# Memory attention and SSM convolution on one core: two stages in a row against one interleaved program

## The chip, the cores and the metric

The kernel runs on one core of one Trainium2 chip. The metric is the device time of one execution in microseconds (us); the median of three runs stands for it. The engines are PE (TensorE, the matrix engine; PEld is its weight load), DVE (VectorE), ACT (ScalarE), POOL (GpSimd) and SP (SyncE), whose queue issues all DMAs of this kernel.

## What is computed

The reference computes two things that don't depend on each other and puts them side by side in the output (1, 2048, 1152), all in bf16.

Part A is attention with a compressive memory: x is 2048 x 576, with 32 heads of 18 channels, in 4 segments of 512 rows.

```
q, k, v = x @ wq, x @ wk, x @ wv            # per head and segment
for s in range(4):
    a_dot = softmax(q_s k_s^T * 18**-0.5 + causal mask) v_s
    a_mem = (phi(q_s) M) / (phi(q_s) z + 1e-6)   # phi(t) = t+1 if t>0 else exp(t)
    o_s   = g * a_mem + (1 - g) * a_dot          # g = sigmoid(beta) per head
    M, z  = M + phi(k_s)^T v_s, z + sum phi(k_s)
out_A = o @ wo
```

Part B is a gated long convolution over 2048 rows and 576 channels: `kv = shift_conv4(k) * v`, `y = causal_conv(kv, ssm_k) + kv * ssm_D`, `out_B = q * y`.

## The kernel before

The entry function runs `part_b` to its end and then `PartA`; each has its own pools. The order on every engine is made by the tile framework: it takes the operations in the order in which the program emits them as priority, and gives buffers from the pools as they come free.

*Part B* (L36 to L307). Tables of sines and cosines are built on DVE and ACT (L91 to L163, helper L28 to L33), seven of 128 x 17 x 128. k and v come in by transposing DMAs (L75, L76); the short convolution is 80 matmuls with diagonal weights (L182), the product with v runs on DVE (L184), and kv goes to a DRAM scratch (L187). The long convolution is a transform of length 4096 = 16 x 256 in matmuls. It runs over NG = 2 groups of GB = 288 channels, each in stages for the whole group: first transform of ssm_k (`f1`, L222, evacuated in turn by DVE L209 and ACT L207), its 17 frequency rows k1 (`f2_mm`, L233 to L240, with a row matmul L237 that adds ssm_D) into H_sb, the same for kv, where each row's product with H_sb goes into Y4 (DVE L259, L262; or ACT L265 and POOL L266), then for all 17 rows the inverse (L272 to L281) into C_sb, transposes (L293), the last small transform (L301) and the product with q (L303). PSUM: 3 tiles of 2 banks and 2 of 1.

*Part A* (L315 to L646). Weights wq and wk are loaded and padded on POOL from 18 to 32 columns a head (`pad_w`, L342 to L348), so that each head starts at a partition that is a multiple of 32. Two heads' groups of four make a pair; there are 4 segments x 4 pairs = 16 slots. `proj_qk` (L419) makes q, k and f = phi(q) of a pair: two blocks each of five matmuls for q (L428) and k (L439), the fifth with 64 rows; `proj_v` (L444) makes v, `proj_phik` (L455) projects k again with rows on partitions and makes phi(k); `mem_update` (L473) sums the memory. `scores` (L489) makes the score blocks (L497), their exp (L501, ACT) and the causal mask (L504, POOL). `av` (L537) multiplies with v (L551) and the memory (L556), evacuates (L553, L557) and normalises: eight DMAs gather the sums (cs, L564), DVE inverts (L573 to L579), eight DMAs write the inverses to DRAM (L585), four read them back broadcast (rb, L588), DVE multiplies (L591 to L594). `out_proj` (L597) multiplies with wo (L604) and stores. `slot` (L617) emits scores of pair i, projections of pair i + 2, `av` of pair i - 1, then the rest. PSUM: 2 tiles of 2 banks for scores, 4 of 1 bank for all else.

Of the kernel before, what the change touches and what calls it, by code (L numbers as in the profile page):

```python
# [13 lines left out]
I32 = dt.int32  # L14
# [21 lines left out]
def part_b(ctx, tc, B_q, B_k, B_v, B_shift_k, B_ssm_k, B_ssm_D, out, GB=288):  # L36
    nc = tc.nc
    ov = out[0].rearrange('(j p) c -> p j c', p=P)
    NG = D // GB
    consts = ctx.enter_context(tc.tile_pool(name="b_consts", bufs=1))  # L40
    ps_mm = ctx.enter_context(tc.tile_pool(name="b_ps_mm", bufs=3, space=PSUM))
    ps_sm = ctx.enter_context(tc.tile_pool(name="b_ps_sm", bufs=2, space=PSUM))

    ident = consts.tile([P, P], BF16)
    nc.gpsimd.memset(ident[:], 0.0)
    nc.gpsimd.affine_select(out=ident[:], in_=ident[:], compare_op=ALU.not_equal, fill=1.0, base=0,
                            pattern=[[-1, P]], channel_multiplier=1)
    pcol_i = consts.tile([P, 1], I32)
    nc.gpsimd.iota(pcol_i[:], pattern=[[0, 1]], base=0, channel_multiplier=1)
    pcol_f = consts.tile([P, 1], F32)  # L50
    nc.vector.tensor_copy(out=pcol_f[:], in_=pcol_i[:])
    pm16_i = consts.tile([P, 1], I32)
    nc.vector.tensor_single_scalar(out=pm16_i[:], in_=pcol_i[:], scalar=15, op=ALU.bitwise_and)
    pm16_f = consts.tile([P, 1], F32)
    nc.vector.tensor_copy(out=pm16_f[:], in_=pm16_i[:])

    ones_row = consts.tile([1, P], BF16)
    nc.vector.memset(ones_row[:], 1.0)
    d_row = consts.tile([1, D], BF16)
    nc.sync.dma_start(out=d_row[:], in_=B_ssm_D.rearrange("(o c) -> o c", o=1))  # L60

    CT0 = [0, 128, 256, 384, 448]
    kv_dram = tc.dram_tile([D, S], BF16, name="kv_scratch")
    kvctx = ExitStack()
    kvp = kvctx.enter_context(tc.tile_pool(name="b_kv", bufs=1))
    sk_bf = kvp.tile([P, 5, 4], BF16)
    for ct in range(5):
        nc.sync.dma_start(out=sk_bf[:, ct, :], in_=B_shift_k[CT0[ct]:CT0[ct] + P, :])
    kTs, vTs = [], []
    for ct in range(5):  # L70
        c0 = CT0[ct]
        kT = kvp.tile([P, KPAD + S], BF16, tag="kT%d" % ct, name="kT%d" % ct)
        vT = kvp.tile([P, S], BF16, tag="vT%d" % ct, name="vT%d" % ct)
        nc.gpsimd.memset(kT[:, 0:KPAD], 0.0)
        nc.sync.dma_start_transpose(out=kT[:, KPAD:KPAD + S], in_=B_k[0, :, c0:c0 + P])  # L75
        nc.sync.dma_start_transpose(out=vT[:, :], in_=B_v[0, :, c0:c0 + P])  # L76
        kTs.append(kT)
        vTs.append(vT)

    genctx = ExitStack()  # L80
    gen = genctx.enter_context(tc.tile_pool(name="b_gen", bufs=1))
    NK1 = 17
    CS = consts.tile([P, NK1, P], BF16)
    SN = consts.tile([P, NK1, P], BF16)
    NSN = consts.tile([P, NK1, P], BF16)
    CST = consts.tile([P, NK1, P], BF16)
    SNT = consts.tile([P, NK1, P], BF16)
    NSNT = consts.tile([P, NK1, P], BF16)
    NCST = consts.tile([P, NK1, P], BF16)
    fpat = gen.tile([P, NK1, P], I32, tag="gen_i")  # L90
    nc.gpsimd.iota(fpat[:], pattern=[[1, NK1], [32, P]], base=0, channel_multiplier=0)  # L91
    prod_f = gen.tile([P, NK1, P], F32, tag="gen_f")
    nc.vector.tensor_scalar(out=prod_f[:], in0=fpat[:], scalar1=pcol_f[:, 0:1], scalar2=None, op0=ALU.mult)
    _trig_from_idx(nc, gen, CS[:], prod_f[:], 1024, 4096, [P, NK1, P], "gen_t")
    _trig_from_idx(nc, gen, SN[:], prod_f[:], 0, 4096, [P, NK1, P], "gen_t")
    _trig_from_idx(nc, gen, NSN[:], prod_f[:], 2048, 4096, [P, NK1, P], "gen_t")
    jpat = gen.tile([P, NK1, P], I32, tag="gen_i")
    nc.gpsimd.iota(jpat[:], pattern=[[0, NK1], [1, P]], base=0, channel_multiplier=0)
    colk_i = consts.tile([P, NK1], I32)
    nc.gpsimd.iota(colk_i[:], pattern=[[1, NK1]], base=0, channel_multiplier=32)  # L100
    colk_f = consts.tile([P, NK1], F32)
    nc.vector.tensor_copy(out=colk_f[:], in_=colk_i[:])
    prodT_f = gen.tile([P, NK1, P], F32, tag="gen_f")
    for k1 in range(NK1):
        nc.vector.tensor_scalar(out=prodT_f[:, k1, :], in0=jpat[:, k1, :], scalar1=colk_f[:, k1:k1 + 1],
                                scalar2=None, op0=ALU.mult)
    _trig_from_idx(nc, gen, CST[:], prodT_f[:], 1024, 4096, [P, NK1, P], "gen_t")
    _trig_from_idx(nc, gen, SNT[:], prodT_f[:], 0, 4096, [P, NK1, P], "gen_t")
    _trig_from_idx(nc, gen, NSNT[:], prodT_f[:], 2048, 4096, [P, NK1, P], "gen_t")
    _trig_from_idx(nc, gen, NCST[:], prodT_f[:], 3072, 4096, [P, NK1, P], "gen_t")  # L110

    k1pat = gen.tile([P, 8, 32], I32, tag="w1_i")
    nc.gpsimd.iota(k1pat[:, :, 0:17], pattern=[[0, 8], [1, 17]], base=0, channel_multiplier=0)
    nc.gpsimd.iota(k1pat[:, :, 17:32], pattern=[[0, 8], [1, 15]], base=1, channel_multiplier=0)
    w1prod = gen.tile([P, 8, 32], F32, tag="w1_f")
    nc.vector.tensor_scalar(out=w1prod[:], in0=k1pat[:], scalar1=pm16_f[:, 0:1], scalar2=None, op0=ALU.mult)
    nc.vector.tensor_scalar(out=w1prod[:, :, 0:17], in0=w1prod[:, :, 0:17], scalar1=8.0, scalar2=None, op0=ALU.add)
    nc.vector.tensor_scalar(out=w1prod[:, :, 17:32], in0=w1prod[:, :, 17:32], scalar1=16.0, scalar2=None, op0=ALU.add)
    W1bd = consts.tile([P, 8, 32], BF16)
    _trig_from_idx(nc, gen, W1bd[:], w1prod[:], 0, 32, [P, 8, 32], "w1_t")  # L120
    nc.gpsimd.affine_select(out=W1bd[:], in_=W1bd[:], compare_op=ALU.is_ge, fill=0.0, base=0,
                            pattern=[[-16, 8], [0, 32]], channel_multiplier=1)
    nc.gpsimd.affine_select(out=W1bd[:], in_=W1bd[:], compare_op=ALU.is_ge, fill=0.0, base=15,
                            pattern=[[16, 8], [0, 32]], channel_multiplier=-1)

    row_i = consts.tile([P, 1], I32)
    nc.vector.tensor_single_scalar(out=row_i[:], in_=pcol_i[:], scalar=2, op=ALU.arith_shift_right)
    row_f = consts.tile([P, 1], F32)
    nc.vector.tensor_copy(out=row_f[:], in_=row_i[:])
    jj_i = consts.tile([P, 1], I32)  # L130
    nc.vector.tensor_single_scalar(out=jj_i[:], in_=pcol_i[:], scalar=3, op=ALU.bitwise_and)
    jj_f = consts.tile([P, 1], F32)
    nc.vector.tensor_copy(out=jj_f[:], in_=jj_i[:])
    rm16_i = consts.tile([P, 1], I32)
    nc.vector.tensor_single_scalar(out=rm16_i[:], in_=row_i[:], scalar=15, op=ALU.bitwise_and)
    rm16_f = consts.tile([P, 1], F32)
    nc.vector.tensor_copy(out=rm16_f[:], in_=rm16_i[:])
    ge17 = consts.tile([P, 1], F32)
    nc.vector.tensor_single_scalar(out=ge17[:], in_=row_f[:], scalar=16.5, op=ALU.is_gt)
    k1r = consts.tile([P, 1], F32)  # L140
    nc.vector.scalar_tensor_tensor(out=k1r[:], in0=ge17[:], scalar=-16.0, in1=row_f[:], op0=ALU.mult, op1=ALU.add)
    offr = consts.tile([P, 1], F32)
    nc.vector.tensor_scalar(out=offr[:], in0=ge17[:], scalar1=8.0, scalar2=8.0, op0=ALU.mult, op1=ALU.add)
    eq0 = consts.tile([P, 1], F32)
    nc.vector.tensor_single_scalar(out=eq0[:], in_=rm16_f[:], scalar=0.5, op=ALU.is_lt)
    ar = consts.tile([P, 1], F32)
    nc.vector.tensor_scalar(out=ar[:], in0=eq0[:], scalar1=-1.0 / 4096.0, scalar2=2.0 / 4096.0, op0=ALU.mult, op1=ALU.add)
    t1pat = gen.tile([P, 4, 16], I32, tag="psi_i")
    nc.gpsimd.iota(t1pat[:], pattern=[[0, 4], [1, 16]], base=0, channel_multiplier=0)
    psiprod = gen.tile([P, 4, 16], F32, tag="psi_f")  # L150
    nc.vector.tensor_scalar(out=psiprod[:], in0=t1pat[:], scalar1=k1r[:, 0:1], scalar2=offr[:, 0:1], op0=ALU.mult, op1=ALU.add)
    psiidx = gen.tile([P, 4, 16], I32, tag="psi_idx")
    nc.vector.tensor_copy(out=psiidx[:], in_=psiprod[:])
# [50 lines left out]
    def eng_copy(out_ap, in_ap):  # L204
        evac_ctr[0] += 1
        if evac_ctr[0] % 2 == 0:
            nc.scalar.copy(out=out_ap, in_=in_ap)  # L207
        else:
            nc.vector.tensor_copy(out=out_ap, in_=in_ap)  # L209
# [481 lines left out]
```

## Time and profile before

| | us |
|---|---|
| three runs | 564.42, 569.20, 576.49 (median 569.2) |
| the profiled execution | 568.13 |
| its span, first to last instruction | 566.4 |
| mean granted TensorE clock | 0.84 |
| PE, DVE, ACT, POOL busy | 431.6, 338.4, 246.6, 145.1 |
| DMA | 33.06 MB, 67,791 packets |

Rows of the timeline give start and length in us, engine, line, operation, what it writes and reads, and how many in a row were merged; square brackets hold the idle time before it and what ended that. Rows of groups give busy time and the mean ns of one, then the idle time before them. "SPq" is the time that the SP queue takes to issue a DMA.

### The profile page before, as it was taken

How to read it: one execution, taken by the hardware profiler on the slowest of the kernel's cores; microseconds unless marked ns; L12 is line 12 of the kernel's file. 1: busy time of each engine (PE TensorE's matmuls, PEld its weight loads, DVE VectorE, ACT ScalarE, POOL GpSimd, SP SyncE). 2: the span in 40 equal slices, each digit the busy share in tenths (PEclk: the TensorE clock that was granted, in tenths of full speed). 3: DMA queues.
4: the chain of work that ended last, by engine and by line, in shares of the span. 5: the costliest groups of instructions: out<-in, count | busy, mean ns of one | idle time of the engine just before them, and what ended most of it. 6: DMA issues, size and time to landing. Idle time of an engine off the chain costs nothing.

```text
span 566.4 us, 8717 instructions
## 1 busy us (share of the span) xinstructions
PE 431.6 (76%) x3329; PEld 202.9 (36%) x3346; DVE 338.4 (60%) x631; ACT 246.6 (44%) x304; POOL 145.1 (26%) x179
## 2 busy tenths in 40 slices
PE   3085877968978735499979979989989999786215
PEld 1033445853446621133423333333424433333103
DVE  6995588373396341245537977467767776654323
ACT  1451443342333400117767853746665568852000
POOL 5000018000054057303333411413233234431000
PEclk9677999995599965669988976999969999967557
DMA  6979430005001035320120111221110211022221
GB/s 134 193 203 254 89 82 4 0 22 148 0 1 48 0 87 138 45 50 2 19 32 21 33 27 19 42 62 50 41 39 15 51 50 52 3 51 61 51 70 48
DMA packets 67791, 33.06 MB, mean 58 GB/s; under 512 B 47461, under 2 KB 65638, under 8 KB 67750
## 3 DMA queue, kind: packets, MB, share of 16 engines
q1 hardware_dynamic: 67750, 32.51, 24.6%
q8 instruction: 26, 0.43, 0.3%
q14 instruction: 15, 0.12, 0.1%
HBM read 17.08 MB, written 7.31 MB: 43 GB/s over the span
## 4 chain that ended last, share of the span: by engine, by line
PE 41%; DVE 24%; DMA 12%; SPq 11%; issue 6%; ACT 5%; DVEq 0%; POOL 0%; ACTq 0%; POOLq 0%
PE pk L439 6%; PE pq L428 5%; PE s L497 5%; DMA rb<-a_r_scratch 4%; SPq L585 4%; SPq L413 4%; PE pout L604 4%; DMA beta<-in_A_beta_dram 3%; DVE Y L259 3%; PE pv L449 3%; DVE A_sb L209 3%; ACT PT L501 2%; PE pkt L463 2%; DVE tmp L32 2%; PE ps L222 2%
## 5 line engine op out<-in xcount | busy, mean ns | idle before, releaser
L501 ACT ACTIVATE PT<-s 128x1024 bf16<-128x1024 f32 x160 | 150.7, 1048 | 87.3 <-PE s L497 83.0
L504 POOL TENSOR_SCALAR_AFFINE_SELECT PT<-PT 128x512 bf16<-128x512 bf16 (+1 forms) x112 | 80.1, 729 | 179.1 <-ACT PT L501 179.1
L604 PE MATMUL pout<-wo_sb,oT 128*128 128x288 bf16 x256 | 42.1, 329 | 35.5 <-DVE oT L594 18.8
L497 PE MATMUL s<-q,k 18*128 18x256 bf16 (+3 forms) x512 | 58.3, 317 | 11.1 <-ACT PT L501 11.1
L428 PE MATMUL pq<-xT,wq_pad 128*128 128x512 bf16 (+1 forms) x145 | 55.6, 436 | 12.8 <-POOL wq_pad L345 10.9
L266 POOL TENSOR_TENSOR Y<-xi_sb,H_sb 128x576 bf16<-128x576 bf16 x22 | 27.6, 1274 | 132.7 <-ACT xi_sb L265 132.3
L439 PE MATMUL pk<-xT,wk_pad 128*128 128x512 bf16 (+1 forms) x159 | 52.6, 420 | 6.4 <-POOL wk_pad L345 3.5
L604 PEld LDWEIGHTS <-oT 128*128 128x128 bf16 x256 | 27.4, 111 | 49.8 <-DVE oT L594 20.8
L449 PE MATMUL pv<-wv_sb,xT 128*128 128x288 bf16 (+1 forms) x160 | 34.0, 337 | 9.0 <-DVE k L441 6.1
L182 PE MATMUL ps<-kT,dg 128*128 128x512 bf16 x79 | 21.6, 435 | 23.7 <-DVE kvT L184 14.9
L593 DVE TENSOR_TENSOR ou<-ou,rb 128x2048 bf16<-128x2048 bf16 x12 | 15.1, 1261 | 38.0 <-DMA rb<-a_r_scratch 38.0
L430 DVE CAST q<-pq 128x512 bf16<-128x512 f32 x32 | 22.0, 688 | 25.1 <-PE pq L428 25.0
L497 PEld LDWEIGHTS <-k 18*128 18x128 bf16 x512 | 17.0, 93 | 55.7 <-issue 53.5
L441 DVE CAST k<-pk 128x512 bf16<-128x512 f32 x32 | 22.0, 689 | 21.2 <-PE pk L439 21.1
L233 PE MATMUL pp<-A_sb,CS 128*128 128x288 bf16 x68 | 22.1, 327 | 12.8 <-ACT xi_sb L265 4.7
L222 PE MATMUL ps<-W1bd,xs 128*128 128x256 bf16 x144 | 23.1, 301 | 9.8 <-DMA xs<-in_B_ssm_k_dram 5.7
L428 PEld LDWEIGHTS <-wq_pad 128*128 128x128 bf16 (+1 forms) x160 | 13.5, 102 | 43.4 <-issue 30.7
L209 DVE CAST H_sb<-pp 128x576 bf16<-128x576 f32 x17 | 12.9, 758 | 25.2 <-PE pp L240 22.3
L207 ACT CAST A_sb<-ps 128x1024 bf16<-128x1024 f32 x18 | 18.1, 1013 | 20.5 <-PE ps L222 20.3
L209 DVE CAST A_sb<-ps 128x1024 bf16<-128x1024 f32 x18 | 21.3, 1220 | 8.0 <-DMA kv_scratch<-kvT 6.2
L551 PE MATMUL po<-PT,V 128*32 128x256 bf16 (+3 forms) x512 | 25.6, 323 | 0.3
L439 PEld LDWEIGHTS <-wk_pad 128*128 128x128 bf16 (+1 forms) x160 | 12.2, 100 | 36.7 <-issue 30.9
(150 smaller groups left out, 727.5 us busy)
## 6 DMA issues: line engine op xcount, KB each, us to landing
rb<-a_r_scratch SPq DMA_DIRECT2D x48, 128.0 KB, 2.7
q_sb<-in_B_q_dram SPq DMA_DIRECT2D x2, 1152.0 KB, 9.8
out_dram<-o_sb SPq DMA_DIRECT2D x2, 1152.0 KB, 6.2
out_dram<-oA SPq DMA_DIRECT2D x16, 144.0 KB, 1.8
kv_scratch<-kvT SPq DMA_DIRECT2D x4, 512.0 KB, 2.6
cs<-ou SPq DMA_DIRECT2D x96, 2.0 KB, 1.8
a_r_scratch<-rb SPq DMA_DIRECT2D x96, 2.0 KB, 1.4
rb<-a_r_scratch SPq DMA_DIRECT2D x16, 64.0 KB, 2.0
```

Of the source, the lines that this page charges most:

```text
L209: nc.vector.tensor_copy(out=out_ap, in_=in_ap)
L222: nc.tensor.matmul(ps[:, u, :], lhsT=xs[:, cc + u, :], rhs=W1bd[:].rearrange("p e k -> p (e k)"), start=True, stop=True)
L266: nc.gpsimd.tensor_tensor(out=Y4[:, k1, 2:4, :], in0=xi_sb[:].unsqueeze(1).to_broadcast([P, 2, GB]), in1=H_sb[:, k1, :, :], op=ALU.mult)
L413: self.nc.sync.dma_start_transpose(out=xT[:, t, :], in_=self.A_x[0, L * s:L * s + L, c0:c0 + P])
L428: nc.tensor.matmul(pq[:], lhsT=self.wq_pad[self.kp(t), t, c:c + P], rhs=xT[self.kp(t), t, :], start=(t == 0), stop=(t == 4))
L439: nc.tensor.matmul(pk[:], lhsT=self.wk_pad[self.kp(t), t, c:c + P], rhs=xT[self.kp(t), t, :], start=(t == 0), stop=(t == 4))
L449: nc.tensor.matmul(pv[:], lhsT=xT[self.kp(t), t, P * tt:P * tt + P], rhs=self.wv[self.kp(t), t, 288 * h:288 * h + 288], start=(t == 0), st ...
L497: nc.tensor.matmul(ps[:, b, off:off + n], lhsT=k[r, u, P * kt:P * kt + P], rhs=q[r, u, P * kt:L], start=True, stop=True, tile_position=(32 ...
L501: nc.scalar.activation(out=dst, in_=ps[:], func=ACT.Exp, scale=self.scale)
L504: nc.gpsimd.affine_select(out=ap, in_=ap, compare_op=ALU.is_ge, fill=0.0, base=0, pattern=pat + [[1, P]], channel_multiplier=-1)
L551: nc.tensor.matmul(po[32 * j:32 * j + 32, P * kt:L], lhsT=V[:, kt, 19 * h:19 * h + 32], rhs=rhs, start=(kt == 0), stop=(kt == 3), tile_pos ...
L604: nc.tensor.matmul(ps[:], lhsT=oT[:, hg % 2, P * qt:P * qt + P], rhs=self.wo[:, hg, 288 * h:288 * h + 288], start=(hg == 0), stop=(hg == 7))
```

## The change

Both parts become classes that share one set of pools, `PartB` as a generator that stops after each small step. The entry function emits attention in 81 steps and, after each, as many of the SSM's 154 steps as keep both in proportion. All of B uses attention's four one-bank PSUM tiles.

- Attention: q and k are projected from dense weights, 9 blocks of 128 columns a segment (`wqk`, a fifth block of 128 rows with zeros); each block goes to a DRAM scratch (10 writes a segment, and 5 of phi(q) in segments 1 to 3), and `load_heads` reads a pair's heads back to partitions 32j (8 DMAs, 12 with phi). phi(k) is read back by four transposing DMAs a segment in place of a second projection. Normalisation gathers with 4 DMAs, writes with 1, reads with 4. Scores and av of a pair are split in halves.
- SSM: groups of GB = 192, NG = 3. Each of 17 frequency rows runs through by itself: H (plus ssm_D on DVE), X (ACT copy), Y (one POOL product of 4 x 192), and the inverse of the row before (evacuated on ACT). Three of seven tables are negated copies. kv is prepared block by block, and q is multiplied in place.

```diff
-    with ExitStack() as bctx:
-        part_b(bctx, tc, B_q, B_k, B_v, B_shift_k, B_ssm_k, B_ssm_D, out)
...
+    b.tables()
+    a.prologue()
+    NB = 10 + NG * (2 * (GB // 8 // 2) + NK1 + 1 + QS // 8)
+    NA = 16 * 5
+    bs, done = b.steps(), 0
+    for i, _ in enumerate(a.steps()):
+        while done < NB * (i + 1) // NA and next(bs, 0) is None:
+            done += 1
...
+        for t in range(5):
+            nc.tensor.matmul(pq[:], lhsT=self.wqk[:, t, 128 * m:128 * m + P], rhs=xT[:, t, :],
+                             start=(t == 0), stop=(t == 4))
+        q = self.pl.stage.tile([P, L], BF16, tag="q", name="q")
+        nc.vector.tensor_copy(out=q[:], in_=pq[:])
...
+            nc.sync.dma_start(out=qd[r0:r0 + P, :], in_=q[:])
...
+        for j in range(4):
+            for k in range(2):
+                nc.sync.dma_start(out=qk[32 * j:32 * j + DH, k, :, :],
+                                  in_=v[k, 8 * p + j:8 * p + j + 5:4].rearrange("u r n -> r u n"))
...
+            nc.sync.dma_start_transpose(out=kt, in_=self.qk_dram[s][D:2 * D, P * tt:P * tt + P])
...
+            self.scores2(s, p)
+            yield
+            if i > 0:
+                self.av((i - 1) // 4, (i - 1) % 4, 1)
+                self.norm((i - 1) // 4, (i - 1) % 4)
+            if s < 3:
+                self.proj_qk(s + 1, PQ[p][0])
+            self.scores(s, p, 0)
+            if s < 3 and p == 0:
+                self.phik(s)
+            yield
+            if s < 3:
+                self.proj_qk(s + 1, PQ[p][1])
+                self.proj_v(s + 1, p)
+            if i + 1 < 16:
+                self.load_heads((i + 1) // 4, (i + 1) % 4) if p < 3 else None
...
+        xs = self.load_xs(self.B_ssm_k, g)
+        A_h = pl.big.tile([P, 32, GB], BF16, tag="big", name="A_h")
+        yield from self.f1(xs, A_h)
...
+        for k1 in range(NK1):
+            ph = self.f2(A_h, k1)
+            Hs = pl.hxy.tile([P, 2, GB], BF16, tag="H", name="Hs")
+            nc.vector.tensor_tensor(out=Hs[:], in0=ph[:], in1=self.DI[:, g, :, :], op=ALU.add)
+            px = self.f2(A, k1)
+            X = pl.hxy.tile([P, 2, GB], BF16, tag="X", name="X")
+            nc.scalar.copy(out=X[:], in_=px[:])
+            Y = pl.hxy.tile([P, 4, GB], BF16, tag="Y", name="Y")
+            nc.gpsimd.tensor_tensor(out=Y[:].rearrange("p (x h) c -> p x h c", x=2),
...
+            if prev is not None:
+                self.inverse(A, *prev)
+            prev = (k1, Y)
+            yield
```

More of the change, by code (lines that the diff above doesn't have):

```diff
@@ L359, in __init__, with late_consts @@
+    def late_consts(self):
+        nc, consts, A_wo = self.nc, self.pl.consts, self.A_wo
+        self.wo = consts.tile([P, 8, D], BF16, name="wo_sb")
         nc.gpsimd.memset(self.wo[:], 0.0)
@@ L406, in kp @@
-    def kp(self, t):
-        return slice(0, P) if t < 4 else slice(64, P)
+        bt = consts.tile([P, H], BF16, name="beta")
+        nc.sync.dma_start(out=bt[:], in_=self.A_beta.partition_broadcast(P))
+        ob = consts.tile([P, H], F32, name="omg")
+        nc.scalar.activation(out=ob[:], in_=bt[:], func=ACT.Exp, scale=1.0)
+        nc.vector.tensor_scalar(out=ob[:], in0=ob[:], scalar1=1.0, scalar2=None, op0=ALU.add)
+        nc.vector.reciprocal(out=ob[:], in_=ob[:])
+        row = consts.tile([P, 1], I32, name="row_a")
```

947 lines of the change are left out of this document (442 added, 505 removed).

## The prediction

> **What bounds the kernel now.** I read the page first (busy shares, then the chain that ended last), then the busy time by stage, then the timeline of one attention slot, and last the groups by line and the DMA issues.
>
> ```profile
> span 566.4 us, 8717 instructions
> PE 431.6 (76%) x3329; PEld 202.9 (36%) x3346; DVE 338.4 (60%) x631; ACT 246.6 (44%) x304; POOL 145.1 (26%) x179
> PE 41%; DVE 24%; DMA 12%; SPq 11%; issue 6%; ACT 5%; DVEq 0%; POOL 0%; ACTq 0%; POOLq 0%
> ...
> 0.00:43.00 43.00, 19.35 (x70) 7.88 (x72) 38.21 (x87) 16.01 (x10) 8.24 (x21) 0.80 0.80 179
> 43.00:204.00 161.00, 130.20 (x983) 82.42 (x982) 96.64 (x127) 57.11 (x83) 27.61 (x22) 0.89 0.23 56
> 204.00:254.00 50.00, 27.12 (x94) 8.73 (x95) 11.90 (x30) 2.72 (x4) 24.20 (x12) 0.58 0.42 90
> 254.00:512.00 258.00, 233.79 (x2062) 92.12 (x2070) 172.23 (x355) 169.42 (x206) 83.17 (x122) 0.91 0.15 34
> 512.00:566.40 54.40, 21.17 (x134) 11.77 (x130) 19.46 (x35) 1.32 (x2) 1.92 (x3) 0.62 0.21 58
> ```
>
> The columns after a stretch's length are the busy time of PE, PEld, DVE, ACT and POOL, then the granted clock. No engine is full over the span. The stages are: SSM tables and the kv product (43 us, DVE), the two SSM groups (161 us), attention start-up (50 us, PE half idle), 16 attention slots (258 us, PE 91% busy), a tail (54 us, PE 39% busy). The program is a row of stages with different limits, and two of them, 104 us, are mostly waiting.
>
> "Busy" counts a matmul's latency, so I price PE by the distance between starts in a dense slot:
>
> ```profile
> 382.98 0.39 PE L497 MATMUL s<-q,k 18*128 18x256 bf16 x4
> 383.30 0.60 PE L428 MATMUL pq<-xT,wq_pad 128*128 128x512 bf16 x2
> ...
> 384.81 1.35 PE L439 MATMUL pk<-xT,wk_pad 128*128 128x512 bf16 x5
> 386.09 0.73 PE L551 MATMUL po<-PT,V 128*32 128x512 bf16 x16
> 386.76 0.39 PE L556 MATMUL pn<-f,Mz_bd 128*128 128x512 bf16 x1
> 387.08 0.73 PE L551 MATMUL po<-PT,V 128*32 128x512 bf16 x16
> 387.74 0.39 PE L556 MATMUL pn<-f,Mz_bd 128*128 128x512 bf16 x1
> 387.96 1.70 PE L449 MATMUL pv<-wv_sb,xT 128*128 128x288 bf16 x10
> 389.60 0.39 PE L497 MATMUL s<-q,k 18*128 18x512 bf16 x4
> 390.35 2.13 PE L604 MATMUL pout<-wo_sb,oT 128*128 128x288 bf16 x16 [0.36 <-DVE ou L553]
> ...
> 95.95 0.29 PE L272 MATMUL pp<-Y,CST 128*128 128x288 bf16 x1
> 96.93 0.29 PE L272 MATMUL pp<-Y,CST 128*128 128x288 bf16 x1
> ```
>
> So a group of four score matmuls costs 0.32 us, a q or k projection of five 1.28, an av block of sixteen 0.67, a pn 0.32, five pv (or pkt) 0.82, sixteen pout 2.13, eight SSM inverse matmuls of 288 columns 0.98 (0.122 each, 0.42 ns a column). For stage 254:512 that gives: 56 q/k projections 72 us, 24 pv and 24 pkt 39, 160 score groups 51, av and pn 27, about 176 of the pout matmuls 23, memory update about 4 (my estimate): about 215 us in 258. **The slots take 1.20 times their PE work.** That ratio carries over into my sum.
>
> **The change part by part.**
>
> *Removed PE work.* Dense q/k projection needs 9 column blocks a segment in place of 16 padded ones; phiK is no longer projected (24 pkt groups, 20 us) but read back transposed; the fifth block becomes a 128-row matmul. Five 512-column matmuls in 1.28 us are 0.26 each; columns alone at 0.42 ns would be 1.08 for five. I take 1.08 to 1.28 for the new groups, 1.1 as the value, since all five now have one shape. Within the slots (segments 1 to 3): 27 groups, 30 us; 24 pv groups at 0.65 to 0.82, 17 us; scores 51; av and pn 29; pout 34; memory update 4. Attention: **165 us**.
>
> *SSM work.* Columns stay the same, in three groups of 192: kv 80x512, first transform 144x256, forward 384x192, inverse 384x192, 144 transposes of 128, 144 of 64. At 0.42 to 0.50 ns a column (the two dense rows above) 253,000 columns are 106 to 126 us; I take **116**. The 34 matmuls of the row d_row go (they are 4 us). Total PE work in the slots 165 + 116 = **281 us**; at 1.20 that is **337 us**.
>
> *The other engines, to see whether one outruns PE.* Rows, mean ns of one after the busy time:
>
> ```profile
> L501 ACT ACTIVATE PT<-s 128x1024 bf16<-128x1024 f32 x160 | 150.7, 1048 | 87.3 <-PE s L497 83.0 <-PE po L551 2.6 <-POOL PT L504 1.7
> L504 POOL TENSOR_SCALAR_AFFINE_SELECT PT<-PT 128x512 bf16<-128x512 bf16 x96 | 62.2, 664 | 164.9 <-ACT PT L501 164.9
> L504 POOL TENSOR_SCALAR_AFFINE_SELECT PT<-PT 128x1024 bf16<-128x1024 bf16 x16 | 17.9, 1119 | 14.2 <-ACT PT L501 14.2
> L266 POOL TENSOR_TENSOR Y<-xi_sb,H_sb 128x576 bf16<-128x576 bf16 x22 | 27.6, 1274 | 132.7 <-ACT xi_sb L265 132.3
> L430 DVE CAST q<-pq 128x512 bf16<-128x512 f32 x32 | 22.0, 688 | 25.1 <-PE pq L428 25.0
> L207 ACT CAST H_sb<-pp 128x576 bf16<-128x576 f32 x17 | 10.8, 638 | 27.7 <-PE pp L240 25.4 <-PE pp L238 2.2
> L265 ACT CAST xi_sb<-pp 128x288 bf16<-128x288 f32 x22 | 8.8, 398 | 23.6 <-DVE Y L259 23.6
> ```
>
> ACT: 160 exps, 151 us; an SSM copy of 384 elements lies between 398 and 638 ns, 0.48 by size; 51 X, 51 C and 36 first-transform copies (0.55) are 69 us, the exps of q and k and the tables 25: **about 245 us**. POOL: the masks stay, 80 us; Y of 768 elements is 1274 x 768/576 = 1.70 us, 51 of them 87 us: **about 170**. In the 54 frequency steps POOL needs 1.70 us and PE 16 x 0.081 = 1.3 a step, so there POOL leads; PE's attention work beside it makes up the difference. DVE: the two Y products leave it for one add a step (51 x 0.55), 28 of 64 q/k casts go, Ct copies come: about **235 us** in the slots. All three stay below 337, so I cost them at nothing while PE or SP sets the pace.
>
> *SP, the DMA queue.* This is where the change adds. Duration min/median/max in ns:
>
> ```profile
> L564 SPq DMA_DIRECT2D cs<-ou x128: 502/588/1591, 287.2 to 542.8; - x128
> L585 SPq DMA_DIRECT2D a_r_scratch<-rb x128: 302/419/526, 293.6 to 549.1; - x128
> L588 SPq DMA_DIRECT2D rb<-a_r_scratch x64: 302/371/1044, 297.6 to 551.0; - x64
> L413 SPq DMA_TRANSPOSE xT<-in_A_x_dram x20: 1124/1258/8778, 204.6 to 356.6; - x20
> L75 SPq DMA_TRANSPOSE kT<-in_B_k_dram x5: 2114/2610/2882, 3.5 to 24.5; - x5
> ...
> xs<-in_B_ssm_k_dram SPq DMA_DIRECT2D x2, 0.2 KB, 8.0
> cs<-ou SPq DMA_DIRECT2D x96, 2.0 KB, 1.8
> a_r_scratch<-rb SPq DMA_DIRECT2D x96, 2.0 KB, 1.4
> rb<-a_r_scratch SPq DMA_DIRECT2D x48, 128.0 KB, 2.7
> ```
>
> Per pair, normalisation drops from 8+8+4 issues to 4+1+4: 9.5 us to 4.3. The head loads (8 or 12 a pair, 176 in all) are not in this trace; between rb's 0.37 and cs's 0.59 they are 65 to 104 us, and I take 0.48, 85 us. Adding 55 scratch writes of q, k and phi(q) at 0.42 (23), normalisation (68), 15 x transposes (19), 12 phiK transposes of like size (17), 10 transposes of k and v (26) and the SSM loads and stores (12): **250 us of issue after the start**. Each pair also waits for cs to land (1.8), for DVE (1.0), for r to land (1.4): 4.2 x 16 = 67 us if nothing is placed between. 317 is below 337, by little; behind a waiting cs stand the next head loads, and for those waits PE.
>
> *Start.*
>
> ```profile
> 213.79 0.58 SPq L338 DMA_DIRECT2D wk_sb<-in_A_wk_dram x1
> 215.42 2.42 PE L428 MATMUL pq<-xT,wq_pad 128*128 128x512 bf16 x5 [10.88 <-POOL wq_pad L345]
> ```
>
> Weights and x land about 13 us in (5 transposes at 1.26, the first loads of wq and wk at 0.58, some 4 to land), 45 matmuls on a cold clock at 0.43 (five take 2.42 with the last one's latency) take 19, scratch write, head loads and their landing 8: **40 us**, between 30 (dense clock) and the 50 of stage 204:254. The tables (part of DVE's 38.2 us in stage 0:43) run beside it.
>
> *Tail.* One normalisation (evacuation 1.4, cs 4 x 0.59 + 1.8, DVE 1.0, r 0.4 + 1.4, rb 4 x 0.37 + 2.7, two products, my estimate 1.9) is 15, the last pout matmuls 8, the store 2: **25 us** in place of 54; now the tail holds three such chains one behind the other.
>
> *New waits.* Each of six xs loads is issued in the step that uses it; two thirds of 8.0 us is 5.3, between 0 (other ready work covers it) and 32 us in all. At three segment ends the first head loads follow the last q/k block through memory, some 6 us each, 0 to 18. I take **12 us** together, a quarter, because attention and SSM each fill the other's gap.
>
> Sum: 40 + 337 + 25 + 12 = 414 us of span. The profiled execution took 568.13 us for 566.4 of span, 1.7 outside; so **416 us** against its 568.1, which is 0.2% under the median of the three runs (569.2).
>
> **The rivals.**
>
> *SP sets the pace.* A slow transfer holds the queue: one x transpose above took 8.8 us to issue, behind eight beta loads. If each of 12 bulk SSM transfers holds SP 6 us, SP needs 317 + 72 = 389 and the time is 40 + 389 + 25 + 12 + 2 = **468 us**. For it: 250 us of issues in some 375 us; against: in the 290 us of the present slots 16 x 9.5 + 19 + 7 = 178 us of issues hid behind PE.
>
> *The two parts don't overlap.* In-order queues and four shared PSUM buffers could make each wait for the other. Then attention's 165 x 1.20 = 198 and the SSM stage's 161 + about 22 for kv add up: 40 + 198 + 183 + 25 = **448 us**. Even this is far below 568, as projection, start and tail shrink by themselves.
>
> *Nearly full overlap.* SP's 317 is the floor, start 32, tail 24: **375 us**.
>
> *Slower: table loads on ACT.* Copies and exps now alternate, and copies ran until now only under the table loaded for Sin:
>
> ```profile
> L33 ACT ACT_TABLE_LOAD x1 | 1.3, 1283 | 0.8 <-PEq L675 0.8
> L401 ACT ACT_TABLE_LOAD x1 | 1.3, 1283 | 29.8 <-DMA beta<-in_A_beta_dram 29.8
> ```
>
> If a copy under Exp's table needed a load, and the next exp another, 138 copies would cost up to 138 x 2 x 1.283 = 354 us: ACT 245 + 354 = 599, time **666 us**. It decides above about 100 of the 138 alternations (ACT past 500 us). No copy follows the second load here, so the trace can't exclude it; that copies ran under Sin's table with no load of their own speaks against it. I give it 3 in 100. The Trainium skill, "ScalarE: Activation LUTs", section "Table sets: the hidden batching unit", says that cheap functions such as copy appear in every set; by that the number of added loads is none and the sum stays as it is. No run here shows it yet for Exp's set.
>
> **How the numbers follow.** Forecast (395 to 440 us) 0.50; SP sets the pace 0.22; no overlap 0.11; nearly full overlap 0.14; table loads 0.03. The ends of the unknown costs (start ±10, head loads ±20, new waits -12 to +38, column price ±12) make 380 to 485; with most of the SP case and some of the full overlap inside, the range is 380 to 490. A difference of 2% is about what a measurement of this kernel tells from no change (its three runs span 564 to 576). Only table loads end above that; so faster 0.96, same 0.01, slower 0.03.
>
> **What would show it.** Right: a first exp before 50 us; PE work of 5 dense projections at 1.1 us; no PE stage under 50% between 45 us and the tail; ACT about 245, POOL about 170, DVE about 270 us busy; two table loads; a tail of about 25 us. SP as the bound would show as waits of scores (L497's successor) for the head loads and SPq high in the chain. Wrong altogether: over two dozen table loads, or two separate stretches of attention and SSM. POOL leading the chain in the frequency steps would mean that I put them beside other work too freely.

## The result and the profile after

The changed kernel takes **512.8 us** (median of four runs, 510.3 to 516.5) against 570.1 for the kernel before on the same chip: ratio 0.903, 95% interval 0.893 to 0.913. The sign was right; the time was not: 416 was forecast, and 512.8 lies above the range of 380 to 490. Some executions of a kernel run in a slower state, and the ratios here and below compare only the others, so they are not always the quotients of the medians. The profiled execution took 514.07 us for a span of 512.2.

From the page of the changed kernel, the busy times and the chain that ended last, by engine and by line:

```profile
span 512.2 us, 8735 instructions
...
PE 359.9 (70%) x3290; PEld 207.4 (40%) x3308; DVE 274.7 (54%) x512; ACT 247.7 (48%) x337; POOL 191.7 (37%) x206
...
PE 40%; DVE 14%; ACT 13%; POOL 11%; DMA 7%; issue 7%; SPq 6%; DVEq 0%; ACTq 0%; POOLq 0%
ACT PT L248 9%; POOL Y L621 9%; PE pq L169 7%; PE pout L344 6%; PE s L244 5%; PE po L299 4%; PE pb L595 4%; SPq L161 3%; PE pb L569 3%; PE pv L205 3%; POOL PT L251 3%; DMA kv<-in_B_k_dram 2%; PE pb L551 2%; DVE Ct L638 2%; PE pb L641 2%
```

PE lost 72 us of busy time, as the dense projection promises, but fell from 76% to 70% of the span: the kernel didn't become a PE-bound one. POOL, which had no share in the chain before, has 11%, 9 of them in one line, the product Y.

The busy time by stretch (columns as before: PE, PEld, DVE, ACT, POOL, granted clock, DMA). The stretches are the start, the kv product, then for each of three SSM groups the first transforms, the 17 frequency rows and the last transforms, then the tail; attention's slots run beside all but the first and last:

```profile
0.00:46.00 46.00, 20.16 (x95) 9.70 (x96) 27.95 (x77) 16.02 (x13) 22.12 (x29) 0.85 0.43 108
46.00:98.00 52.00, 31.18 (x163) 12.12 (x160) 24.57 (x58) 15.75 (x19) 6.66 (x11) 0.82 0.91 201
98.00:138.00 40.00, 33.29 (x381) 15.74 (x384) 25.00 (x47) 28.54 (x38) 11.14 (x18) 0.88 0.36 92
138.00:205.00 67.00, 51.17 (x436) 32.41 (x437) 31.26 (x49) 39.27 (x63) 39.60 (x33) 0.83 0.33 77
205.00:223.00 18.00, 14.82 (x275) 10.01 (x273) 12.14 (x21) 6.55 (x7) 4.76 (x9) 0.70 0.20 57
223.00:278.00 55.00, 43.32 (x342) 21.62 (x348) 34.73 (x67) 32.57 (x42) 10.82 (x16) 0.85 0.46 112
278.00:343.00 65.00, 47.73 (x535) 31.86 (x539) 34.14 (x54) 36.51 (x59) 41.87 (x36) 0.89 0.27 75
343.00:362.00 19.00, 15.81 (x187) 11.22 (x186) 12.89 (x21) 5.71 (x6) 3.55 (x4) 0.94 0.34 82
362.00:403.00 41.00, 31.30 (x244) 13.72 (x242) 28.11 (x47) 28.86 (x36) 9.52 (x15) 0.80 0.41 105
403.00:468.00 65.00, 47.95 (x444) 32.95 (x444) 23.59 (x41) 36.01 (x56) 40.47 (x34) 0.84 0.18 48
468.00:486.00 18.00, 10.62 (x126) 7.92 (x125) 11.69 (x18) 1.94 (x2) 1.22 (x2) 0.78 0.14 39
486.00:512.20 26.20, 12.53 (x89) 8.11 (x88) 8.62 (x16) 0.00 (x0) 0.00 (x0) 0.75 0.26 74
```

Half of what was gained lies in the tail, 54.4 us before and 26.2 now. What took 469 us before (the two SSM groups, attention's start-up and its slots) takes 440 here, from 46 to 486 us, with the kv product in it.

The stretches of frequency rows are the longest, 67 + 65 + 65 = 197 us for 51 rows. In them no engine is full: PE is busy 75% of the time, POOL 62%, ACT 57%. The same holds for the kv stretch (PE 60%), except that its DMA engines are 91% busy. The waits name who stands for whom:

```profile
ACT PT L248 <- PE po L299: 47.2, 9, 15.2
ACT PT L248 <- PE s L244: 43.0, 42, 4.9
...
PE pb L595 <- POOL Y L621: 41.2, 29, 3.8
PE s L244 <- ACT PT L248: 25.6, 40, 1.3
...
POOL Y L621 <- ACT X L619: 23.9, 12, 4.7
```

(us in all, times, longest.) These are loops. PE stands at an inverse for the Y of its row, Y stands for the copy X, and X for PE. Y leads the chain within each of the three stretches of rows, with 18%, 21% and 28% of it. ACT's exps stand for scores of PE, and PE's scores for the exps. The program fixes the order on every engine, so each wait also holds what stands behind it: attention's matmuls behind a waiting inverse, X and C copies behind a waiting exp.

### The profile page after: what moved, and what is told of

The parts are those of the page before. It is cut to its first block, busy times and chain, and to the rows that moved or that the text cites. A ratio compares the mean times of both kernels' runs of the same rounds, so it can differ in the third digit from the quotient of the medians.

```text
span 512.2 us, 8735 instructions
## 1 busy us (share of the span) xinstructions
PE 359.9 (70%) x3290; PEld 207.4 (40%) x3308; DVE 274.7 (54%) x512; ACT 247.7 (48%) x337; POOL 191.7 (37%) x206
## 4 chain that ended last, share of the span: by engine, by line
PE 40%; DVE 14%; ACT 13%; POOL 11%; DMA 7%; issue 7%; SPq 6%; DVEq 0%; ACTq 0%; POOLq 0%
ACT PT L248 9%; POOL Y L621 9%; PE pq L169 7%; PE pout L344 6%; PE s L244 5%; PE po L299 4%; PE pb L595 4%; SPq L161 3%; PE pb L569 3%; PE pv L205 3%; POOL PT L251 3%; DMA kv<-in_B_k_dram 2%; PE pb L551 2%; DVE Ct L638 2%; PE pb L641 2%
## 5 line engine op out<-in xcount | busy, mean ns | idle before, releaser
L621 POOL TENSOR_TENSOR Y<-X,Hs 128x768 bf16<-128x768 bf16 x51 | 88.4, 1749 | 30.6 <-ACT X L619 23.9
L244 PE MATMUL s<-qk 18*128 18x384 bf16 (+3 forms) x512 | 66.5, 339 | 33.6 <-ACT PT L248 25.6
L169 PE MATMUL pq<-xT,wqk 128*128 128x512 bf16 x165 | 56.9, 460 | 15.2 <-DMA wqk<-in_A_wk_dram 12.6
L595 PE MATMUL pb<-Y,CST 128*128 128x192 bf16 x141 | 29.1, 256 | 43.6 <-POOL Y L621 41.2
L616 DVE TENSOR_TENSOR Hs<-pb,DI 128x384 bf16<-128x384 f32 x51 | 28.1, 553 | 33.0 <-PE pb L584 24.7
L619 ACT CAST X<-pb 128x384 bf16<-128x384 f32 x51 | 24.3, 484 | 25.5 <-PE pb L584 24.7
L299 PE MATMUL po<-PT,V 128*32 128x128 bf16 (+3 forms) x512 | 32.7, 352 | 3.4 <-issue 1.6
L205 PE MATMUL pv<-wv,xT 128*128 128x288 bf16 x160 | 25.9, 315 | 12.7 <-DVE V L207 10.3
L569 PE MATMUL pb<-W1bd,xs 128*128 128x256 bf16 x144 | 27.0, 302 | 4.7 <-DMA xs<-in_B_ssm_k_dram 3.7
L551 PE MATMUL pb<-kv,dg 128*128 128x512 bf16 x77 | 21.4, 420 | 11.1 <-DMA kv<-in_B_k_dram 10.6
L595 PE MATMUL pb<-Y,NSNT 128*128 128x192 bf16 x147 | 26.8, 262 | 0.0
```

What stands on the lines that cost most here:

```text
L169: nc.tensor.matmul(pq[:], lhsT=self.wqk[:, t, 128 * m:128 * m + P], rhs=xT[:, t, :], start=(t == 0), stop=(t == 4))
L205: nc.tensor.matmul(pv[:], lhsT=xT[:, t, P * tt:P * tt + P], rhs=self.wv[:, t, 288 * h:288 * h + 288], start=(t == 0), stop=(t == 4))
L244: self.nc.tensor.matmul(ps[:, b, off:off + n], lhsT=qk[r, 1, u, P * kt:P * kt + P], rhs=qk[r, 0, u, P * kt:L], start=True, stop=True, tile ...
L299: nc.tensor.matmul(po[32 * j:32 * j + 32, P * kt:L], lhsT=V[:, kt, 19 * h:19 * h + 32], rhs=rhs, start=(kt == 0), stop=(kt == 3), tile_pos ...
L551: nc.tensor.matmul(ps[:], lhsT=dg[:, i, :], rhs=t[:, 0, o:o + 512], start=(i == 0), stop=(i == 3))
L569: nc.tensor.matmul(ps[:, u, :], lhsT=xs[:, cc + u, :], rhs=self.W1[:].rearrange("p e k -> p (e k)"), start=True, stop=True)
```

## The experiments

Time is the median; the ratio is to runs of the kernel before on the same chip (medians 569.5 to 576.7), with its interval. Runs without a ratio are single executions, so a few us between two of them say nothing. The changed kernel stands at 512.8 and 0.903.

| run | us | ratio (interval) |
|---|---|---|
| e1 inverse two rows behind | 484.7 | 0.847 (0.835 to 0.858) |
| e5 Y in halves | 494.6 | 0.871 (0.860 to 0.882) |
| e6 both | 473.3 | 0.833 (0.825 to 0.842) |
| e2 plain kv loads | 507.2 | 0.888 (0.879 to 0.897) |
| e3 attention alone | 366.5 | |
| e4 SSM alone | 272.6 | |
| e7 attention alone, projection twice | 384.7 | |
| e8 e1 with projection twice | 495.0 | 0.871 (0.864 to 0.879) |
| e9 attention alone, whole-slot lead | 346.6 | |
| e11 attention alone, exps spread | 365.0 | |
| e12 e6 with exps spread | 464.3 | 0.816 (0.809 to 0.823) |
| e10 attention alone, no head loads | 314.7 | |
| e13 changed kernel, no head loads | 491.9 | 0.865 (0.862 to 0.868) |
| e16 e12, no head loads | 440.1 | 0.774 (0.768 to 0.779) |
| e14 attention alone, q and k early | 361.7 | |
| e15 e12, q and k early | **456.4** | 0.803 (0.799 to 0.807) |
| e17 attention alone, loads by ACT | 384.9 | |
| e18 e12, loads by ACT | 460.3 | 0.809 (0.805 to 0.812) |

**The frequency rows.** Theory: a row is a chain f2, X, Y, inverse, and one row of distance is too little for it once attention stands in the same queues. Rival: POOL's rate.

```diff
-            if prev is not None:
-                self.inverse(A, *prev)
-            prev = (k1, Y)
+            if len(prev) == 2:
+                self.inverse(A, *prev.pop(0))
+            prev.append((k1, Y))
```

> The inverse transform is issued two frequency rows behind its product instead of one (a third Y buffer; three small tiles moved to make room). Chain theory: in the changed kernel the three frequency phases (17 rows each) take 67 + 65 + 65 = 197 us, and in 41 us of them PE stands before an inverse for the Y of the row before; with another row of distance most of that goes, so the phases fall to about 160 us and the time from 513 to 475 to 485 us. GpSimd-rate theory (Y at 1.75 us and the masks beside it set the pace): Y and masks still come as often as before, so the phases stay near 195 us and the time near 510. If the waits only move to attention's exp and its PV products, 500 to 510.

e5 leaves the distance and divides the product:

```diff
-            nc.gpsimd.tensor_tensor(out=Y[:]..., in0=X[:]..., in1=Hs[:]..., op=ALU.mult)
+            for x, eng in ((0, nc.gpsimd), (1, nc.vector)):
+                eng.tensor_tensor(out=Y[:, 2 * x:2 * x + 2, :], in0=X[:, x:x + 1, :].to_broadcast([P, 2, GB]),
+                                  in1=Hs[:], op=ALU.mult)
```

> The changed kernel with the product Y in two halves: GpSimd makes the half with the real part of X, VectorE the other at the same time. Chain theory: the step that every inverse waits for shrinks from 1.75 us to some 0.9 on GpSimd, so the 41 us of waits for Y go down by half or more and the time falls from 513 to 485 to 495. GpSimd-rate theory: GpSimd loses 43 us of work in those phases, the time falls by as much or more, to 470 or below. Rival: VectorE, which in the frequency phases also has the Hs adds and attention's casts, becomes what is late, and the two engines slow each other when both read SBUF: 505 to 520.

> The inverse two rows behind and Y in two halves, together. If both remove the same wait: no better than the two-row kernel alone, 480 to 487. If a rate of GpSimd is still left after the first: below 475. If VectorE becomes late: above 490.

Measured: 485, 495 and 473. In the two-row kernel POOL does the same work, and yet 28 us go. They go where the edit is: from the first to the last H add of a group, the three groups together take 172 us in the changed kernel and 138 in this one (132 with both edits). Rows of its waits, then of the groups of Y (the changed kernel's first), then the wait that is left with both edits:

```profile
PE pb L594 <- POOL Y L620: 11.3, 9, 2.5
```

```profile
L621 POOL TENSOR_TENSOR Y<-X,Hs 128x768 bf16<-128x768 bf16 x51 | 88.4, 1749 | 30.6 <-ACT X L619 23.9
L620 POOL TENSOR_TENSOR Y<-X,Hs 128x768 bf16<-128x768 bf16 x51 | 87.8, 1745 | 13.7 <-DVE Hs L615 9.2 <-ACT X L618 4.3
```

```profile
PE pb L594 <- POOL Y L621: 5.6, 5, 1.9
```

The wait for Y went from 41.2 to 11.3 us with Y as long as ever (1.745 us against 1.749), so the distance was the cause of these 28 us and POOL's rate was not. Halving Y shortens the same chain and does part of the same: 18 us alone, some 11 more on top of e1 (8 by the ratios; their intervals still touch). By its expectation, e6 below 475 would mean that a rate of POOL is still left; 473 is just below, and these runs don't tell rate from chain for that last part. The rival in which DVE becomes late fell by the time, but Y's wait for DVE's H rose from 9.2 us in e1 to 21.4 in e6.

**The kv product.**

```diff
-        nc.sync.dma_start_transpose(out=t[:, 0, KPAD:KPAD + S], in_=self.B_k[0, :, CT0[ct]:CT0[ct] + P])
+        nc.sync.dma_start(out=t[:, 0, KPAD:KPAD + S], in_=self.B_k[0].rearrange("(p a) c -> p (a c)", p=P)[:, 0:S])
```

(and the same for B_v)

> Leaves out the transposition of B_k and B_v: the ten transposing loads of 128 x 2048 become plain loads of the same bytes, so the convolution works on wrongly ordered data. Transposing loads as the bound of the kv phase (52 us from 46 to 98, DMA engines 91% busy): the phase falls to about 35 us and the time by 12 to 17, to some 498. Rival (attention's first slots set the pace there, the loads are hidden): 508 to 515.

507, just under the rival's 508 to 515; the intervals of e2 and of the changed kernel touch. The first H add starts at 131.0 us in its trace and at 138.5 in that of the changed kernel. The transposing loads cost some 6 us (9 by the ratios), if anything. What else makes this stretch 52 us long (slot 1 waits for x of segment 1, whose only buffer is held to the end of the prologue) was not tried.

**Each part alone.** The loop that emits both is replaced by one over one part's steps.

> Leaves out the whole SSM branch after its tables (its output columns are not written). By the terms of the prediction: start 40, attention's 165 us of PE work at the ratio 1.20, tail 25: about 265 us. If attention in its new form (heads through DRAM, row by row) has a chain of its own that is longer than its work: 300 or more, and then interleaving can't be blamed for all of the slots' length.

> Leaves out attention after its prologue (its output columns are not written). Chain theory: per row Y 1.65 us runs beside inverse 0.65, f2 0.65, the X copy 0.48 and some 0.5 us of signalling of the next rows, about 2.3 us a row, 51 rows 117 us, against 197 beside attention, so most of the extra 80 us is attention's work put into the same queues. GpSimd-rate theory: 1.7 us a row, 87 us. If the rows take 3 us or more alone, the SSM stream's own chain is the cause, with no part of attention's. Whole time 40 + 40 (kv) + 117 + some 75 for first and last transforms = about 270 us.

The stretch from the first to the last exp of attention alone, and three stretches of the SSM alone (the kv product with group 0's first transforms; its 17 frequency rows; its last transforms with group 1's first):

```profile
34.00:336.00 302.00, 239.32 (x1869) 90.90 (x1869) 145.17 (x283) 178.92 (x191) 84.27 (x126) 0.68 0.31 82
```

```profile
46.00:87.00 41.00, 30.30 (x147) 14.70 (x146) 25.43 (x55) 7.27 (x13) 0.22 (x2) 0.89 1.07 232
87.00:120.00 33.00, 24.27 (x246) 21.71 (x244) 8.92 (x16) 15.20 (x33) 27.47 (x17) 0.95 0.12 23
120.00:152.00 32.00, 20.24 (x160) 15.01 (x159) 17.18 (x26) 7.62 (x14) 0.08 (x1) 0.63 0.36 79
```

The SSM alone meets its expectation: 33 us for 17 rows, 1.94 a row, between the two theories' 1.7 and 2.3 (no row shows the latter's 0.5 us of signalling as such; here Y starts 0.08 us after X ends); beside attention, whose work is emitted between them, the same rows take 3.86. Attention alone is the surprise: 302 us of slots where the forecast's terms have 165 x 1.20 = 198. That is longer than the 258 us of the slots' stage before, which held more PE work (215). So attention's new form has a chain of its own that is longer than its work, and the mixing alone can't be blamed.

**The clock.** In attention alone the granted clock is 0.68, in the slots of the kernel before it was 0.91. Perhaps the projection work that went had kept it up:

```diff
+        for t in range(5 if s > 0 else 0):
+            nc.tensor.matmul(pq[:], lhsT=self.wqk[:, t, 128 * m:128 * m + P], rhs=xT[:, t, :],
+                             start=(t == 0), stop=(t == 4))
```

> Leaves out the SSM branch as in the run of attention alone, and computes the q and k projection of segments 1 to 3 twice into the same bank (27 x 5 extra matmuls of 512 columns, 29 us at full clock, the result unchanged). Attention alone took 366.5 us at a granted clock of 0.71. Clock theory (the dense projection took away the work that kept TensorE's clock up, so the rest runs slower): the granted clock rises to 0.8 or more and the time stays at 345 to 370 in spite of the work. Work theory (TensorE's queue is the pace): 366 + 29 / 0.71 = 395 to 410. Chain theory of attention (exps and head loads set the pace, TensorE has room): 366 to 375 with the clock about where it was.

> The two-row kernel with the q and k projection of segments 1 to 3 computed twice (29 us of TensorE work at full clock, the result unchanged). Work theory: 485 + 29 / 0.844 = about 519. Clock theory: the clock rises above 0.87 and the time stays within 475 to 495. Chain theory (TensorE has room): 485 to 500, clock unchanged.

385 at a clock of 0.755, and 495 at 0.872 (e1: 0.844). Each theory is half right: 29 us of added dense work raised the clock and cost 18 and 10 us (the latter is 14 by the ratios). By the medians, two thirds of the added work cost nothing in the whole kernel; how much of that is room on PE and how much the higher clock is not separated. More PE work never paid.

**The exps' lead.** The kernel before emitted ten exps of a slot first and their PV products a slot later; the changed one has three score buffers and two to four exps ahead. e9 gives attention alone the old order (eight buffers, two for x). e11 and e12 keep the buffers and deal the exps out evenly:

```diff
     def scores(self, s, p, u):
...
+        self.T[s, p, "PT", u] = (p0, None)
+
+    def scores1(self, s, p, u):
+        p0 = self.T[s, p, "PT", u][0]
+        p1 = self.pl.pt.tile([P, 4, L], BF16, tag="PT", bufs=3, name="PT1")
...
             yield
+            self.scores1(s, p, 0)
             if s < 3:
                 self.proj_qk(s + 1, PQ[p][1])
...
             yield
+            self.scores1(s, p, 1)
             if s < 3 and p == 1:
                 self.mem_update(s)
```

> Leaves out the SSM branch, as the run of attention alone (366.5 us, 18.7 us a slot). Attention's steps in the order of the kernel before: all ten exps of a slot first, then projections, and the PV products one whole slot later, with eight score buffers instead of three and two x buffers. Theory of the lead (the changed kernel's exps have a lead of two only, so ScalarE and TensorE wait for each other in turns): 366 falls to 310 to 335. Theory of the clock alone (less projection work, lower clock): little change, 355 to 370. Theory of the head loads: little change too.

> Leaves out the SSM branch. Same buffers as the changed kernel, but the ten exps of a slot are dealt out 2, 2, 2, 2, 2 over its five steps instead of 2, 4, 0, 4, 0, so the last two no longer wait for the first PV's buffers and TensorE's long blocks (projection, V, out projection) have exps beside them. Lead theory: 366 falls to 335 to 350. Clock or load theory: 360 to 370.

> Whole kernel: two rows of distance, Y in halves, and the exps dealt out 2, 2, 2, 2, 2. Lead theory: the 45 us in which ScalarE's exps stand before PV and part of the 30 + 37 us of TensorE and ScalarE waiting for each other go, 473 falls to 435 to 455. If attention's order costs nothing once SSM work fills the gaps: 468 to 476. If the exps, now between the X and C copies of every row, delay these: above 478.

e9 took 20 us off, less than I expected; e11 none. The lead is at most a part of it (e9 also adds an x buffer and moves the projections). In the interleaved kernel the spread did pay, 473 to 464, less than the lead theory's 435 to 455. ACT's wait for PV products went from 44.5 us in e6 to 25.7, but its wait for scores rose from 36.6 to 51.0, and the rows of the SSM didn't get shorter (132 and 131 us from first to last H adds), so these waits don't show where the 9 us went:

```profile
ACT PT L247 <- PE po L298: 44.5, 8, 14.5
ACT PT L247 <- PE s L243: 36.6, 36, 4.6
```

```profile
ACT PT L247 <- PE s L243: 51.0, 35, 8.5
ACT PT L247 <- PE po L302: 25.7, 6, 15.1
```

**The head loads.** `load_heads` returns at once after the sixth slot, and by the second half of its condition for the third and fourth slots too: 136 of the 176 loads, those of 12 slots and not of ten, are left out.

```diff
+        if 4 * s + p > 5 or s == 0 and p > 1:
+            return
```

> Leaves out the SSM branch and, after the sixth slot, the loads of q, k and phi(q) rows from DRAM, so later slots compute with stale heads. Head-load theory: the 21 us in which score weights wait for these loads and the SP queue's share go, 366 falls to 340 or below. Lead theory and clock theory: 360 to 368.

> The changed kernel, leaving out the loads of q, k and phi(q) rows after the sixth slot (later slots compute with stale heads). In attention alone these loads were worth 52 us over ten slots. If they hold attention back here as well: 513 falls to 460 to 480. If the SSM's work fills the time in which a slot waits for its heads (TensorE waits only 18 us for such loads in the trace of the changed kernel): 495 to 512.

> The best kernel so far, leaving out the loads of q, k and phi(q) rows after the sixth slot. It bounds what any better order of these loads can bring: if the slots wait for heads here, 415 to 440; if another wait takes their place, 450 to 464.

Here is more than half of attention's missing time: 366 falls to 315, a slot from 18.9 us to 15.3 (198 / 16 = 12.4 was forecast), and the clock rises from 0.68 to 0.79 by itself:

```profile
34.00:278.00 244.00, 201.60 (x1869) 82.17 (x1869) 144.22 (x278) 173.01 (x191) 92.58 (x126) 0.79 0.30 78
```

In the interleaved kernels the same loads cost 21 us (513 to 492, between the two theories) and 24 us (464 to 440, the end of the first theory's range). Beside the SSM's work they cost less than half as much. The trace of attention alone shows the direct part, weight loads of the scores and scores that wait for such a row:

```profile
PEld L244 <- DMA qk<-a_qk_scratch: 20.9, 18, 2.2
PE s L244 <- DMA qk<-a_qk_scratch: 8.6, 11, 1.9
```

Is it the SP queue, where the loads stand behind normalisation's transfers that wait for DVE, or the loads themselves?

```diff
             self.scores2(s, p)
+            if p < 3:
+                self.load_heads(s, p + 1, (0, 1))     # q and k rows; phi(q) stays where it was
```

> Leaves out the SSM branch. The q and k rows of the next slot are loaded from DRAM one step earlier, ahead of the norm's transfers on the SP queue instead of behind them; phi(q) stays. Queue-order theory (the loads are late because they stand behind transfers that wait for VectorE): 366 falls to 325 to 345, most of the way to the 315 without loads. If the loads cost by themselves (their 264 transfers of 18 rows x 2 KB on the queue and on the DMA engines): 355 to 366.

(The trace has 176 such loads, 128 of q and k and 48 of phi(q), not 264.)

> The best kernel so far (two rows of distance, Y in halves, exps spread; 464 us) with q and k rows loaded ahead of the norm's transfers. Queue-order theory: 440 to 455. If SSM work hides the loads or the loads cost by themselves: 460 to 468.

```diff
-                nc.sync.dma_start(out=qk[32 * j:32 * j + DH, k, :, :],
+                nc.scalar.dma_start(out=qk[32 * j:32 * j + DH, k, :, :],
```

> Leaves out the SSM branch. The loads of q, k and phi(q) rows are issued by ScalarE instead of SyncE, so they no longer stand behind transfers that wait for VectorE; the transfers themselves are the same. Queue-order theory: 366 falls to 320 to 345, although ScalarE now issues some 176 transfers at about 0.32 us. If the loads cost by themselves (rows, DMA engines, landing time): 355 to 370.

> The whole kernel with two rows of distance, Y in halves and the exps spread (464 us), with the head loads issued by ScalarE. Leaving out these loads gave 440. Queue-order theory: 440 to 456. If ScalarE's 56 us of issuing delay the exps and the copies of the frequency rows as much as the queue did: 460 to 472.

e15 gains 8 us and is the fastest kernel of all that compute the whole, 456.4, a ratio of 0.803; e18 gains 4, within its interval. In attention alone neither move helped: 362, a change no larger than the spread of one kernel's executions (564 to 576 before), and 385 with the loads on ACT. Three rows (of e3, e14 and e17) say why these don't decide it. In e14 SP stands longer for normalisation's r than before (27.3 us in e3), and what was moved ahead of one r stands behind the one before it; in e17 the exps stand on ACT behind the loads:

```profile
SPq L324 <- DVE r L322: 27.3, 13, 4.7
```

```profile
SPq L326 <- DVE r L324: 53.7, 13, 9.2
```

```profile
ACT PT L248 <- DMA qk<-a_qk_scratch: 23.1, 6, 6.9
```

So it is shown that the loads of these 12 slots cost 21 to 24 us in the interleaved kernels, and open how much of this is their place in a queue and how much their own time.

## Why the prediction was wrong, point by point

*Right.* The amounts of work: ACT 247.7 us busy (245 forecast), POOL 169.6 and DVE 238.1 between 46 and 486 us (170 and 235). Five projection matmuls, by the row below, are 4 starts in 1.24 - 0.39 us, 0.21 each, 1.06 for five (1.1). The tail is 26.2 us (25). The first exp comes at 33.9 us (before 50); the start is 46 us against 40.

```profile
227.38 1.24 PE L169 MATMUL pq<-xT,wqk 128*128 128x512 bf16 x5
```

*The table loads.* Five, not two, but all in the start, where Sin and Exp alternate; the copies among the exps behind them need none. That rival is gone, as the Trainium skill, "ScalarE: Activation LUTs", section "Table sets: the hidden batching unit", has it.

```profile
L449 ACT ACT_TABLE_LOAD x2 | 2.6, 1283 | 0.0
L248 ACT ACT_TABLE_LOAD x2 | 2.6, 1283 | 0.0
L121 ACT ACT_TABLE_LOAD x1 | 1.3, 1283 | 0.8 <-PEq L684 0.8
```

*The step that failed: "The slots take 1.20 times their PE work. That ratio carries over into my sum."* It doesn't. The stretch from 46 to 486 us is 440 for the same 281 us of work, 1.57. With 12 for new waits the forecast had 349 there, so this step holds 91 of the 98 us by which the profiled execution (514.1) missed; the start holds 6. By the row below PE is busy for 327 of the 440 us and stands still for 113; at the ratio of the slots before (233.8 busy for 215 of work in 258 us) 281 us of work would be 306 busy and 31 still, and 12 more for the new waits. So some 70 of the 91 us are PE standing still, which is what the experiments went after. The other 21 are longer matmuls. That is about what the granted clock's fall from 0.91 to 0.84 would make (306 x 0.91 / 0.84 = 331), but it isn't shown to be the cause.

```profile
46.00:486.00 440.00, 327.20 (x3115) 189.57 (x3128) 238.10 (x420) 231.72 (x325) 169.61 (x177) 0.84 0.38 93
```

The ratio belonged to one stage: one stream, ten exps ahead, eight score buffers and heads that came straight from PE through DVE. The change took all of these away. The parts alone show it: attention 302 / 165 = 1.83, the SSM (46 to 271) 225 / 116 = 1.94. Interleaving did hide work, 302 + 225 = 527 in 440, but from a far higher level than 198 + 183.

The range failed with the step: its ends were set by the start, the head loads, the new waits and the price of a column, and even all four at their worst are 416 + 80 = 496 (all at their best 362; neither is the 485 or the 380 that was written), because the ratio itself had no range.

What the runs put in place of the ratio, each on top of the one before:

| what | us | shown by |
|---|---|---|
| chain of the frequency rows, one row of distance | 28 | e1 |
| the same chain, Y of 1.75 us | 11 | e6 (touches e1's interval) |
| exps dealt out evenly | 9 | e12 |
| head loads through DRAM, 12 of 16 slots | 24 | e16 |

These are differences of medians from different chips; by the ratios the four are 32, 8, 10 and 24 us. Either way it is some 73 of the 97 us between the medians, down to 440. Of the remaining 24, 6 are the start, and the kv loads are some 6 to 9, if anything (measured on the changed kernel alone); the rest is open. Even with all four edits, the span of 437.7 us less the same start and tail is 366, a ratio of 1.30. No run gave the SSM PSUM tiles of its own; between 46 and 486 us PE waits only some 4 us for evacuations by DVE or ACT, besides the exps and Ct, so this rival is small by the trace and untested by a run.

*"POOL leads; PE's attention work beside it makes up the difference."* This costed the rows at nothing, because 1.70 us of POOL and 1.3 of PE a row are both below what PE has to do. But a row is a loop over three engines, and e1 shows that its turn was set here by latency and distance: POOL's work was the same, and the rows took 138 us in place of 172. The prediction named this sign of its own failure, POOL leading the chain in the frequency steps; it came.

*Head loads.* I priced them by the issue, 0.48 us each; the issue is cheaper than that, and the cost lies with whoever waits for the rows:

```profile
L194 SPq DMA_DIRECT2D qk<-a_qk_scratch x128: 266/321/715, 24.1 to 442.1; - x128
```

*The rival "SP sets the pace"* had this place right (a load behind a waiting transfer, PE behind the load) and the mechanism wrong: it laid the price on bulk SSM transfers. *"The two parts don't overlap"* took 198 for attention from the same failed ratio.

## What to carry to other kernels

A ratio of time to work is a property of one schedule: how far ahead each producer is emitted and how many buffers it has. When a change cuts buffers or lead, or sends data through DRAM, follow one turn of each loop over the engines and price its latency against the distance, even if every engine has room. Before interleaving two streams in in-order queues, lengthen the distance in their loops: here one row more of lookahead and one buffer were worth 28 us, while an even order of attention's exps brought 9.

## What the runs showed of the hardware

*TensorE's clock falls without a long idle stretch.* In attention alone, between 260 and 320 us, PE is busy 78% and never idle for more than 1.9 us, and the granted clock is 0.59; in the SSM's rows above it is busy 74% at 0.95. The 0.59 is a mean: the clock on record is 1 or 0.5, and it stays at 0.5 for 30.7 us, from 277.4 to 308.1, in which no idle stretch of PE is longer than 1.2 us.

```profile
260.00:320.00 60.00, 46.55 (x289) 14.85 (x289) 25.82 (x42) 37.67 (x39) 18.44 (x27) 0.59 0.28 80
```

The Trainium skill, "TensorE: Matmul & The Clock Gate", section "What's actually happening", ties the half clock to an idle window of some 3.4 us; this trace shows the half clock with shorter gaps. Attention's score and PV matmuls there use 18 rows or 32 columns of the array, the SSM's all 128; whether that is the reason was not tried.

*GpSimd and VectorE slow each other.* Y takes 1.631 to 1.640 us in the SSM alone; beside attention up to 2.62, and the last add of the normalisation, 0.69 us as a rule, took 2.02 beside two Ys of 4.21 together. Three of its twelve ran beside a Y and took 1.65, 1.66 and 2.02 us; the nine others took 0.68 to 0.69 (min/median/max in ns, then two rows of the timeline, all of the changed kernel; the last fence is the SSM alone):

```profile
L621 POOL TENSOR_TENSOR Y<-X,Hs x51: 1629/1635/2620, 145.0 to 464.8; 128x768 bf16<-128x768 bf16 x51
...
L334 DVE TENSOR_TENSOR oT<-ou x12: 675/692/2017, 221.8 to 501.2; 128x1024 bf16<-128x1024 bf16 x12
```

```profile
291.02 4.21 POOL L621 TENSOR_TENSOR Y<-X,Hs 128x768 bf16<-128x768 bf16 x2 [0.59 <-ACT X L619]
...
293.77 2.02 DVE L334 TENSOR_TENSOR oT<-ou 128x1024 bf16<-128x1024 bf16 x1
```

```profile
L621 POOL TENSOR_TENSOR Y<-X,Hs x51: 1631/1636/1640, 87.2 to 248.0; 128x768 bf16<-128x768 bf16 x51
```

Both operations read two operands from SBUF. The Trainium skill, "SBUF — State Buffer", section "Who interferes with whom", says that such a VectorE instruction contends with a GpSimd instruction that reads SBUF; the rows agree. It costs little here: Y's median is that of the SSM alone, and all 51 take 88.4 us where 51 of 1.636 are 83.4.
